# Q/K stacks of 16-row pieces, second tiles from token 768, and ten x tiles loaded during attention

## The chip, the core and the metric

The kernel runs on one core of a Trainium2 chip. Its engines work side by side: TensorE (PE; its weight loads are PEld), VectorE (DVE), ScalarE (ACT), GpSimd (POOL) and SyncE (SP), which here issues all DMA transfers, in an order written out by hand. The metric is device microseconds of one launch; lower is better.

## What is computed

A transformer block on x of 2048 tokens by 640, in float32: a layer norm, sliding-window attention, and a gated MLP that mixes over tokens.

```python
qkv = layernorm(x) @ wqkv                   # 32 heads of 20
scores = q @ k.T * 20 ** -0.5               # key at most 255 tokens back, not ahead
h = x + (softmax(scores) @ v) @ wo
z = gelu(layernorm(h) @ w_in)               # 640 -> 2 x 864
g = w_sp @ layernorm(z[:, 864:]) + b_sp     # over the 2048 tokens
out = h + (z[:, :864] * g) @ w_out
```

## The kernel before

Float32 products are made from pieces: a number is split into a high and a low part (`split`), and three products of parts are added up. For Q and K the parts are three bfloat16 numbers; six pairs of parts, 20 rows each, stand one above another in 120 rows, a *stack*, so that one bfloat16 matmul over 120 rows gives a score.

First the v projection, then Q and K. `qk_item(m, c)` makes block m (of 10, 128 rows each) for 512 tokens c; `split_qk` makes its three parts in `sg` (VectorE, ScalarE, GpSimd) and SP stores them to `qk_d` in DRAM (L619). `load_stack(g)` loads the stack of four heads (group g of 8) into one of three slots: two halves of 1024 tokens, 12 transfers of 20 rows each, every sixth row (L329). Slot 2 lies in `xb`, which held the normalized x.

Attention runs in 128 steps s, 16 to a group. `max_item` (L345) makes scores of 32-query strips and lets VectorE take their row maxima: one reduction (L369) that writes a throw-away tile `junk`, from a ring of two, and reads out the maximum into a column of `m_cols`. It runs 18 steps (`LEAD`) ahead of `score_item` (L391), which makes the transposed scores with the maxima as three more rows, and ScalarE's exponential. `max_rows` turns 32 columns of maxima and sends them through DRAM into the slot (L384, L386). `pv_item` (L425) multiplies by v; `o_d` gets the result through a ring of six tiles `ot` (L462). Where a window of keys or queries crosses token 1024, `tokens` cuts the matmul in two. Steps 0 to 109 have maxima and scores; the first 18 units of maxima run beside the last Q/K items, and in the last 18 steps no maxima are left.

Every engine but GpSimd takes its instructions in program order (`manual_schedule`). The waits between them follow from the tiles: a tile of a ring is reused when its last users are done, and reads and writes of the same bytes are ordered.

`last_steps` has what is done at the end of a step: from 117 on the first loads of the projection (`load_sums`, `load_o`), and the x tiles (`load_x2`) and half of w_in's first columns (`load_win_half`) from 121. `proj_early` loads the split wo. Then follow 16 tiles of `proj_o`, with `add_h` (h = x + projection, stored to `h_d`), a layer norm, and `turn_h` (stored to `hn_d`), while `win1_prep` splits w_in. The gated MLP follows, in a list of steps.

Of the kernel before, what the change touches and what calls it, by code (L numbers as in the profile page):

```python
# [34 lines left out]
def block_kernel(ctx, tc, x, xt, wqk, wv, wo, w_in, wsp, bsp, w_out, out):  # L35
# [16 lines left out]
    qk_d = dram.tile([2, 3, 2, 2 * DH, H // 2, S // 4], F32, name="qk_d")  # L52
# [73 lines left out]
    def open_early(pl):  # L126
# [4 lines left out]
        mem["xh"] = [pl.tile([P, D], F32, name=f"xh{i}") for i in range(6)]  # L131
        mem["ho"] = [pl.tile([P, D], F32, name=f"ho{i}") for i in range(3)]
        mem["wraw"] = pl.tile([P, 2, 2, HF], F32, name="wraw")
# [27 lines left out]
    def load_x2(i):  # L161
        hs[i] = mem["xh"][i % 6]
        nc.sync.dma_start(hs[i], x[i * P:(i + 1) * P, :])
# [75 lines left out]
    def ready(i):  # L239
# [7 lines left out]
        121: lambda: (load_x2(0), load_win_half(0, 0), load_x2(1), inverse_load(1), load_win_half(0, 1), ready(0)),  # L247
        122: lambda: first_sums(1),
        126: lambda: (ready(1), inverse_recip(1), inverse_store(1), load_o(2), inverse_load(2), load_x2(2)),
        127: lambda: (ready(2), norm_o(3), load_sums(2)),  # L250
        128: lambda: (split_o(3, True)(), inverse_recip(2), load_sums(3), inverse_store(2), load_o(3)),
        129: lambda: (load_x2(3), load_x2(4)),
    }


    with ExitStack() as ab:
# [7 lines left out]
        xb = [xb.tile([P, CH], F32R, name=f"xb{i}") for i in range(2)]  # L264
        s0 = pool(low0, "slot0p")
        s0 = [s0.tile([P, 2 * S], F32R, name=f"slot0_{i}") for i in range(2)]
# [12 lines left out]
        add_slot(2, [h[:, :2 * S] for h in xb])  # L279
# [36 lines left out]
        def load_stack(g):  # L316
# [3 lines left out]
            if g < 3:  # L320
                for h in st:
                    nc.gpsimd.memset(h[96:P, 1], ONES)
                    if g == 2:
                        yield
            for b in range(2):
                for j, parts in enumerate(((0, 0), (0, 1), (0, 2), (1, 0), (1, 1), (2, 0))):
                    for a in range(2):
                        src = qk_d[g // 4, parts[a], b, a * DH:(a + 1) * DH, g % 4 * 4:g % 4 * 4 + 4]
                        nc.sync.dma_start(st[b][j:6 * DH:6, a], src)  # L329
                        yield  # L330

        def tokens(st, rows, a, hh, t0, n):

            o = 0
            while o < n:
                c, t = divmod(t0 + o, S // 2)
                w = min(n - o, S // 2 - t)
                yield o, w, st[c][:rows, a, hh, t:t + w]
                o += w

        def one(st, rows, a, hh, t0, n):
            (_, _, x), = tokens(st, rows, a, hh, t0, n)
            return x

        def max_item(g, qb, hh, strips=True):  # L345
# [4 lines left out]
            n = (qb + 1) * P - lo  # L350
            keep = mask[:, 384 - n:]
            if strips:
# [3 lines left out]
                for j in range(4):  # L356
                    q0 = qb * P + 32 * j
                    for o, w, k in tokens(st, 120, 1, hh, lo + skip * j, n):
                        nc.tensor.matmul(ps[32 * j:32 * j + 32, o:o + w], one(st, 120, 0, hh, q0, 32), k,  # L359
                                         start=True, stop=True, tile_position=(0, 32 * j))  # L360
            else:
                for o, w, k in tokens(st, 120, 1, hh, lo, n):
                    nc.tensor.matmul(ps[:, o:o + w], one(st, 120, 0, hh, qb * P, P), k, start=True, stop=True)  # L363
# [3 lines left out]
            junk = tmp2.tile([P, 384], BF16, tag="junk", bufs=2, name=f"junk{g}_{qb}_{hh}")  # L367
# [4 lines left out]
        def max_rows(g, b):  # L372
# [13 lines left out]
            nc.sync.dma_start(slot_w[g % 3][b][120:123, 0], rows.rearrange("a (h r) c -> a h (r c)", h=4))  # L386
# [4 lines left out]
        def score_item(u, hh):  # L391
# [14 lines left out]
            for i in range(4):  # L406
# [4 lines left out]
                for o, w, q in tokens(st, 123, 0, hh, kb * P + b, e - b):  # L411
                    nc.tensor.matmul(ps[32 * i:32 * i + 32, b + o:b + o + w], one(st, 123, 1, hh, k0, 32), q,  # L412
                                     start=True, stop=True, tile_position=(0, 32 * i))
# [51 lines left out]
        if True:  # L465
# [3 lines left out]
            def load_x(i):  # L469
                xts[i] = tmp.tile([P, D], F32, tag="ta", bufs=3, name=f"xt{i}")  # L470
# [6 lines left out]
            def load_xt(i):  # L477
                tag, bufs = ("wql", 4) if i % 3 == 2 else ("tb", 2)
                xns[i] = tmp.tile([P, KD, P], F32, tag=tag, bufs=bufs, name=f"xt_t{i}")
# [18 lines left out]
            def xn_tile(i):  # L498
                return tmp.tile([P, D], F32, tag="tb", bufs=2, name=f"xn{i}")
# [6 lines left out]
            def store_std():  # L506
                ps = s2_tile()[:NT, :P]
                nc.tensor.transpose(ps, inv_std, ident)
                row = tmp.tile([NT, P], F32, tag="std", bufs=2, name="std_row")
# [44 lines left out]
            def load_wqk(m):  # L554
                raws[m] = tmp.tile([P, KD, P], F32, tag="wraw", bufs=3, name=f"wqraw{m}")
# [10 lines left out]
            def load_wo(k):  # L566
                raws[k] = tmp.tile([P, D], F32, tag="wraw", bufs=3, name=f"woraw{k}")
# [16 lines left out]
            def load_std(c):  # L584
                stds[c] = tmp.tile([P, 512], F32, tag="std", bufs=2, name=f"std{len(stds)}_{c}")
# [17 lines left out]
            def split_qk(m, c, ps):  # L603
                sg = tmp.tile([P, 3, 512], BF16, tag="ta", bufs=3, name=f"sg{m}_{c}")
                rest = tmp.tile([P, 512], F32, tag="tb", bufs=2, name=f"rest{m}_{c}")
# [11 lines left out]
                T = S // 4  # L617
# [945 lines left out]
```

## Time and profile before

| | us |
|---|---|
| median of 3 runs | 1105.15 (1104.84 to 1106.06) |
| the profiled execution | 1106.78 |
| its span | 1105.1 |
| attention with maxima and scores | 240.0 to 437.6 of the span |
| last attention steps | 437.6 to 462 |
| output projection, first norm | 462 to 547 |

In the profile L12 is line 12 of the kernel, `out<-in` are tiles without their numbers, `xN` counts instructions, and "idle before" is time in which the engine did nothing ahead of an instruction, with what ended it. "issue" is a wait that no semaphore explains. A row of a timeline has start, duration, engine, line and operation; a row of waits has the total, the number of times and the longest.

### The profile page before, as it was taken

The page shows a single profiled execution, that of the slowest core. Times are in us where ns is not written, and L with a number is a line of the kernel's source. Part 1 is how long each engine was busy: PE and PEld are TensorE (multiplying, and loading weights), DVE is VectorE, ACT ScalarE, POOL GpSimd, SP SyncE. Part 2 cuts the span into 40 slices and gives each one's busy share as a digit, 9 for nine tenths or more (in the row PEclk, how much of TensorE's full clock was granted, in tenths as well). Part 3 has the DMA queues.
Part 4 walks back from the last instruction along what each step waited for, and adds up shares of the span by engine and source line. Part 5 has one row for each costly group of instructions (what it writes and reads, how often), then busy time and mean ns, then how long its engine had stood idle before and what let it go on. Part 6 is the DMA issues. An engine that isn't in the chain of part 4 may idle for free.

```text
span 1105.1 us, 28747 instructions
## 1 busy us (share of the span) xinstructions
PE 1075.2 (97%) x11059; PEld 968.4 (88%) x11059; DVE 781.0 (71%) x2157; ACT 604.7 (55%) x1258; POOL 314.0 (28%) x447
## 2 busy tenths in 40 slices
PE   8999999999999999999999999999999999999998
PEld 8998886658888787699999998999999899999998
DVE  6643445779999897575677668655556899987684
ACT  4443443249999899756766556443458433333331
POOL 4324446677766666721200012000001000000000
PEclk9999999999999999999999999999999999999999
DMA  7834657555565565689655342242441467684642
GB/s 252 296 115 118 175 172 262 169 181 171 190 188 189 178 192 151 183 263 296 252 184 174 131 142 77 66 133 97 127 148 51 173 223 254 229 276 137 195 141 96
DMA packets 92281, 194.73 MB, mean 176 GB/s; under 512 B 11952, under 2 KB 46272, under 8 KB 88256
## 3 DMA queue, kind: packets, MB, share of 16 engines
q1 hardware_dynamic: 92144, 192.90, 53.4%
q8 instruction: 87, 1.43, 0.6%
q14 instruction: 50, 0.41, 0.1%
HBM read 127.90 MB, written 64.95 MB: 175 GB/s over the span
## 4 chain that ended last, share of the span: by engine, by line
PE 79%; DMA 6%; ACT 4%; DVE 4%; issue 4%; POOL 2%; SPq 1%; DVEq 0%; POOLq 0%; ACTq 0%
PE g L1181 23%; PE pv L440 6%; PE bank L359 5%; PE bank L412 5%; PE zb L1066 4%; PE qk L592 4%; PE qk L594 4%; PE qk L593 4%; PE out_x L1345 3%; PE zx L1006 2%; PE out_v L1345 2%; PE zv L1006 2%; DMA h_d<-xh 1%; PE zy L1006 1%; PE zw L1006 1%
## 5 line engine op out<-in xcount | busy, mean ns | idle before, releaser
L415 ACT ACTIVATE pt<-bank 128x384 f32<-128x384 f32 (+1 forms) x452 | 180.2, 483 | 17.2 <-PE bank L412 10.8
L1181 PE MATMUL g<-zl,aw 128*128 128x432 f32 x768 | 169.1, 357 | 1.5 <-ACT zl L828 1.0
L369 DVE CUSTOM_DVE_ANT_0 junk<-bank,strip 128x288 bf16<-128x288 f32 x392 | 156.1, 452 | 12.3 <-PE bank L359 10.1
L828 ACT ACTIVATE aw<-fx 128x512 fp32r<-128x512 f32 (+2 forms) x152 | 86.2, 587 | 127.6 <-DVE fx L822 57.9
L1181 PEld LDWEIGHTS g<-zl,aw 128*128 128x128 f32 x768 | 144.0, 188 | 8.1 <-ACT zl L828 1.4
L440 PE MATMUL pv<-pt,v_sb 128*32 128x192 f32 (+3 forms) x1984 | 135.2, 322 | 4.6 <-POOL pt L419 2.4
L822 DVE TENSOR_TENSOR aw<-fx,aw 128x512 fp32r<-128x512 f32 (+2 forms) x152 | 95.8, 638 | 60.1 <-ACT aw L828 59.8
L1181 PE MATMUL g<-ze,aw 128*128 128x432 f32 x576 | 132.6, 359 | 2.3 <-DVE row L822 2.3
L1181 PEld LDWEIGHTS g<-ze,aw 128*128 128x128 f32 x576 | 107.1, 188 | 9.0 <-DVE row L822 3.7
L419 POOL TENSOR_SCALAR_AFFINE_SELECT pt<-pt 128x512 f32<-128x512 f32 x128 | 83.5, 653 | 61.2 <-ACT pt L415 59.0
L412 PE MATMUL bank<-slot 123*32 123x288 bf16 (+8 forms) x1296 | 95.7, 273 | 2.0 <-issue 1.3
L359 PE MATMUL bank<-slot 120*32 120x288 bf16 (+6 forms) x1248 | 93.5, 275 | 0.9 <-DVE mcol L369 0.8
L440 PEld LDWEIGHTS pv<-pt,v_sb 128*32 128x32 f32 x1984 | 65.5, 110 | 11.9 <-POOL pt L419 6.2
L422 POOL TENSOR_SCALAR_AFFINE_SELECT pt<-pt 128x512 f32<-128x512 f32 x112 | 71.2, 635 | 0.0
L412 PEld LDWEIGHTS <-slot 123*32 123x32 bf16 x1728 | 58.8, 96 | 13.0 <-issue 3.6
L359 PEld LDWEIGHTS <-slot 120*32 120x32 bf16 x1408 | 52.1, 95 | 15.2 <-issue 7.2
L369 DVE CUSTOM_DVE_ANT_0 junk<-bank,mask 128x384 bf16<-128x384 f32 (+2 forms) x120 | 51.2, 444 | 17.0 <-PE bank L363 15.7
L822 DVE TENSOR_TENSOR row<-g,row 128x432 f32<-128x432 f32 x80 | 48.3, 603 | 21.0 <-PE g L1181 20.6
L616 POOL TENSOR_TENSOR sg<-rest,sg 128x512 bf16<-128x512 f32 x40 | 46.7, 1167 | 56.3 <-ACT sg L615 45.6
L606 DVE TENSOR_TENSOR rest<-qk,std 128x512 f32<-128x512 f32 x40 | 27.6, 690 | 44.9 <-PE qk L594 44.9
L608 ACT ACTIVATE sg<-rest 128x512 bf16<-128x512 f32 x40 | 25.2, 631 | 54.3 <-DVE rest L606 54.3
L118 PE MATMUL wo_ps<-xb,xb 128*128 128x320 f32 x260 | 52.4, 311 | 1.5 <-DVE mvc L1460 1.5
(263 smaller groups left out, 2538.4 us busy)
## 6 DMA issues: line engine op xcount, KB each, us to landing
slot<-qk_d SPq DMA_DIRECT2D x144, 160.0 KB
fx<-wsp_in SPq DMA_DIRECT2D x32, 512.0 KB
qk_d<-sg SPq DMA_DIRECT2D x40, 384.0 KB
o_d<-ot SPq DMA_DIRECT2D x64, 128.0 KB
xb<-qk_d SPq DMA_DIRECT2D x48, 160.0 KB
fx<-hn_d SPq DMA_DIRECT2D x24, 320.0 KB
z_d<-row SPq DMA_DIRECT2D x16, 432.0 KB
g_d<-row SPq DMA_DIRECT2D x16, 432.0 KB
```

Of the source, the lines that this page charges most:

```text
L359: nc.tensor.matmul(ps[32 * j:32 * j + 32, o:o + w], one(st, 120, 0, hh, q0, 32), k, start=True, stop=True, tile_position=(0, 32 * j))
L369: nc.vector.tensor_tensor_reduce(out=junk[:, :n], in0=ps[:, :n], in1=keep, scale=1.0, scalar=NEG, op0=OP.add, op1=OP.max, accum_out=m_cols ...
L412: nc.tensor.matmul(ps[32 * i:32 * i + 32, b + o:b + o + w], one(st, 123, 1, hh, k0, 32), q, start=True, stop=True, tile_position=(0, 32 * i))
L415: nc.scalar.activation(pt[:, hh, :n], ps[:, :n], AF.Exp, scale=SCALE)
L419: nc.gpsimd.affine_select(out=pt[:, :, :P], in_=pt[:, :, :P], pattern=[[0, 4], [1, P]], base=0, channel_multiplier=-1, compare_op=OP.is_ge ...
L422: nc.gpsimd.affine_select(out=pt[:, :, 256:], in_=pt[:, :, 256:], pattern=[[0, 4], [-1, P]], base=-1, channel_multiplier=1, compare_op=OP. ...
L440: nc.tensor.matmul(ps[32 * hh:32 * hh + 32, a - 512 * c:b - 512 * c], v_sb[:, kb, v0:v0 + 32], pt[:, hh, a - kb * P:b - kb * P], start=fir ...
L822: (eng or nc.vector).tensor_tensor(out=out, in0=a, in1=b, op=op)
L828: nc.scalar.activation(out, a, AF.Copy)
L1006: nc.tensor.matmul(ps, a[x], b[:, y], start=start and m + x + y == 0, stop=stop and m == n - 1 and x == 1, skip_group_check=True)
L1181: nc.tensor.matmul(ps, w[m][:, x, k], zc[k][m][:, y], start=start and k + x + y == 0, stop=stop and k == 3 and x == 1, skip_group_check=True)
L1345: nc.tensor.matmul(o[b][:, :HD], l[:, x, k * P:(k + 1) * P], r[k][:, y], start=start and k + x + y == 0, stop=stop and k == 2 and x == 1, ...
```

## The change

The rows of Q and K in the weights are reordered: of each head's 20 rows, the first 16 make eight blocks, the last 4 two more. A stack now has six pieces of 16 rows and one of 24 (the six times 4 last rows, which `split_qk` stores six times, as often as the pairs use them). The second tile of a stack starts at token 768 and holds 1280 tokens; the first keeps 1024. So no window crosses a seam, and `tokens` is gone. The three rows of maxima follow the two tiles.

A scratch `raw`, kept through attention, takes the place of several rings of the first stage (`tmp_of` counts them out). From step 66 it takes ten x tiles, each in two transfers of 64 rows, and from 106 w_in's first piece in transfers of 32 rows. The wo loads go in halves. The store of h is issued after the loads of its step. The ring of `junk` has one tile instead of two.

```diff
-    qk_d = dram.tile([2, 3, 2, 2 * DH, H // 2, S // 4], F32, name="qk_d")
+    WORDS = (S // 4, S // 4 + P)
+    qk_d = [dram.tile([2, 2, 3, 16, H // 2, n], F32, name=f"qk_d{b}") for b, n in enumerate(WORDS)]
+    qr_d = [dram.tile([2, 2, 6, DH - 16, H // 2, n], F32, name=f"qr_d{b}") for b, n in enumerate(WORDS)]
+    PAIRS = ((1, 0), (0, 1), (0, 0), (0, 2), (2, 0), (1, 1))
...
     def load_x2(i):
-        hs[i] = mem["xh"][i % 6]
-        nc.sync.dma_start(hs[i], x[i * P:(i + 1) * P, :])
+        hs[i] = mem["xh"][i % 10]
+        for r in ((slice(0, 64), slice(64, P)) if i < 10 else (slice(0, P),)):
+            nc.sync.dma_start(hs[i][r], x[i * P:(i + 1) * P][r])
...
-        nc.sync.dma_start(mem["wraw"][:, b], src[r:r + P])
+        for o in range(0, P, 32):
+            nc.sync.dma_start(mem["wraw"][o:o + 32, b], src[r + o:r + o + 32])
...
-                nc.sync.dma_start(wo_s[p][:, k].bitcast(F32), wo_d[k, p])
+                for r in (slice(0, 64), slice(64, P)):
+                    nc.sync.dma_start(wo_s[p][r, k].bitcast(F32), wo_d[k, p, r])
...
-        121: lambda: (load_x2(0), load_win_half(0, 0), load_x2(1), inverse_load(1), load_win_half(0, 1), ready(0)),
+        121: lambda: (inverse_load(1), ready(0)),
...
-        126: lambda: (ready(1), inverse_recip(1), inverse_store(1), load_o(2), inverse_load(2), load_x2(2)),
+        126: lambda: (ready(1), inverse_recip(1), inverse_store(1), load_o(2), inverse_load(2)),
...
-        129: lambda: (load_x2(3), load_x2(4)),
+        129: lambda: load_win(2),
     }
+    for i in range(10):
+        last_steps[66 + 4 * i] = lambda i=i: load_x2(i)
+    for b in range(2):
+        last_steps[106 + 4 * b] = lambda b=b: load_win_half(0, b)
...
+        raw = pool(base_stack, "raw").tile([P, 10 * D + 2 * FH], F32, name="raw")
+        mem["xh"] = [raw[:, i * D:(i + 1) * D] for i in range(10)]
+        mem["wraw"] = view(raw, 10 * D, 2, 2, HF)
...
-        s0 = [s0.tile([P, 2 * S], F32R, name=f"slot0_{i}") for i in range(2)]
+        s0 = [s0.tile([P, 8 * n], F32R, name=f"slot0_{i}") for i, n in enumerate(WORDS)]
...
+            q, heads = g // 4, slice(g % 4 * 4, g % 4 * 4 + 4)
             for b in range(2):
-                for j, parts in enumerate(((0, 0), (0, 1), (0, 2), (1, 0), (1, 1), (2, 0))):
+                for j, parts in enumerate(PAIRS):
                     for a in range(2):
-                        src = qk_d[g // 4, parts[a], b, a * DH:(a + 1) * DH, g % 4 * 4:g % 4 * 4 + 4]
-                        nc.sync.dma_start(st[b][j:6 * DH:6, a], src)
+                        nc.sync.dma_start(st[b][16 * j:16 * j + 16, a], qk_d[b][q, a, parts[a], :, heads])
                         yield
+                for a in range(2):
+                    nc.sync.dma_start(st[b][96:6 * DH, a], qr_d[b][q, a, :, :, heads].rearrange("j d h t -> (j d) h t"))
+                    yield
...
-                    for o, w, k in tokens(st, 120, 1, hh, lo + skip * j, n):
-                        nc.tensor.matmul(ps[32 * j:32 * j + 32, o:o + w], one(st, 120, 0, hh, q0, 32), k,
-                                         start=True, stop=True, tile_position=(0, 32 * j))
+                    nc.tensor.matmul(ps[32 * j:32 * j + 32, :n], one(st, half_b, 120, 0, hh, q0, 32),
+                                     one(st, half_b, 120, 1, hh, lo + skip * j, n),
+                                     start=True, stop=True, tile_position=(0, 32 * j))
...
-            junk = tmp2.tile([P, 384], BF16, tag="junk", bufs=2, name=f"junk{g}_{qb}_{hh}")
+            junk = tmp2.tile([P, 384], BF16, tag="junk", bufs=1, name=f"junk{g}_{qb}_{hh}")
...
+            if b == 0:
+                nc.sync.dma_start(st[0][120:123, 0], rows)
+                nc.sync.dma_start(st[1][120:123, 0, :, :P], rows[:, :, 6 * P // 2:])
+            else:
+                nc.sync.dma_start(st[1][120:123, 0, :, P:], rows)
...
-                for o, w, q in tokens(st, 123, 0, hh, kb * P + b, e - b):
-                    nc.tensor.matmul(ps[32 * i:32 * i + 32, b + o:b + o + w], one(st, 123, 1, hh, k0, 32), q,
-                                     start=True, stop=True, tile_position=(0, 32 * i))
+                c = int(kb > 5)
+                nc.tensor.matmul(ps[32 * i:32 * i + 32, b:e], one(st, c, 123, 1, hh, k0, 32),
+                                 one(st, c, 123, 0, hh, kb * P + b, e - b),
+                                 start=True, stop=True, tile_position=(0, 32 * i))
...
-                xts[i] = tmp.tile([P, D], F32, tag="ta", bufs=3, name=f"xt{i}")
+                xts[i] = tmp_of("ta")[:, :D]
...
+                for b in range(2):
+                    t0, t1 = max(c * 256, 3 * P * b), min(c * 256 + 256, (3 * P + WORDS[1]) if b else WORDS[0])
...
+                    if m % 5 < 4:
...
+                        nc.sync.dma_start(bass.AP(tensor=base.tensor, offset=base.offset,
+                                                  ap=[[W, P], [16 * n * W, 3], [1, t1 - t0]]), part)
+                        continue
+                    for a in range(2):
+                        for p in range(3):
+                            js = [j for j, x in enumerate(PAIRS) if x[a] == p]
...
-            for _ in range(1 + s % 2 if s >= NT else 2 * min(s, 1)):
+            for _ in range(1 + (s % 4 > 0) if s >= NT else 2 * min(s, 1)):
                 next(ld, None)
...
-        nc.sync.dma_start(h_d[i], hs[i])
+        return hs[i]
...
-        if i == 1:
-            load_win(2)
-        if 1 < i < NT - 3:
-            load_x2(i + 3)
+        if 2 < i < NT - 7:
+            load_x2(i + 7)
+        nc.sync.dma_start(h_d[i - 1], hx)
```

The calls of `load_stack`'s pieces in the first stage go from three to four at a time.

More of the change, by code (lines that the diff above doesn't have):

```diff
@@ L278, in block_kernel @@
         add_slot(0, s0)
-        add_slot(2, [h[:, :2 * S] for h in xb])
+        add_slot(2, [h[:, :8 * n] for h, n in zip(xb, WORDS)])
         mask = tmp2.tile([P, 384], BF16, name="mask")
@@ L357, in max_item @@
                     q0 = qb * P + 32 * j
[L358 to L363 removed]
+                    nc.tensor.matmul(ps[32 * j:32 * j + 32, :n], one(st, half_b, 120, 0, hh, q0, 32),
+                                     one(st, half_b, 120, 1, hh, lo + skip * j, n),
+                                     start=True, stop=True, tile_position=(0, 32 * j))
+            else:
+                nc.tensor.matmul(ps[:, :n], one(st, half_b, 120, 0, hh, qb * P, P), one(st, half_b, 120, 1, hh, lo, n),
+                                 start=True, stop=True)
             b, c = divmod(qb, 8)
@@ L498, in xn_tile @@
             def xn_tile(i):
-                return tmp.tile([P, D], F32, tag="tb", bufs=2, name=f"xn{i}")
+                return tmp_of("tb")
             def mean_row(i):
@@ L508, in store_std @@
                 nc.tensor.transpose(ps, inv_std, ident)
-                row = tmp.tile([NT, P], F32, tag="std", bufs=2, name="std_row")
+                row = tmp_of("std")[:NT, :P]
                 nc.scalar.activation(row, ps, AF.Copy)
@@ L566, in load_wo @@
             def load_wo(k):
[L567 removed]
+                raws[k] = tmp_of("wraw")
                 nc.sync.dma_start(raws[k], wo[k * P:(k + 1) * P, :])
@@ L718, in block_kernel @@
                 if n >= 20:
-                    for _ in range(3):
+                    for _ in range(4):
                         next(ld0, None)
@@ L730, in dense_tail @@
                         s1 = pool(x01, "slot1p", side="right")
-                        add_slot(1, [s1.tile([P, 2 * S], F32R, name=f"slot1_{i}") for i in range(2)])
+                        add_slot(1, [s1.tile([P, 8 * n], F32R, name=f"slot1_{i}") for i, n in enumerate(WORDS)])
                     if n >= 7:
-                        for _ in range(3):
+                        for _ in range(4):
                             next(ld1, None)
@@ L739, in block_kernel @@
                 if n % 5 == 4:
-                    for _ in range(3):
+                    for _ in range(4):
                         next(ld0, None)
@@ L752, in block_kernel @@
                     next(rows)
-            assert next(dense, 0) == 0 and next(ld0, 0) == 0
+            assert next(dense, 0) == 0 and next(ld0, 0) == 0 and next(ld1, 0) == 0
             for _ in after[0]:
@@ L1544 @@
     w = np.asarray(A_wqkv).reshape(D, 3, H, DH)
-    wqk = w[:, :2].reshape(D, 2, 2, H // 2, DH).transpose(2, 1, 4, 0, 3).reshape(2 * D // P, 8, KD, P, H // 2)
+    wqk = w[:, :2].reshape(D, 2, 2, H // 2, DH).transpose(2, 1, 4, 0, 3)
+    wqk = np.concatenate([wqk[:, a, d] for d in (slice(0, 16), slice(16, DH)) for a in range(2)], axis=1)
+    wqk = wqk.reshape(2 * D // P, 8, KD, P, H // 2)
     wqk = wqk.transpose(0, 3, 2, 1, 4).reshape(2 * D // P, P, KD, P)
```

58 lines of the change are left out of this document (33 added, 25 removed).

## The prediction

> **What bounds the kernel now.** I read the busy shares of the page first, then the stretches of the span, then, for the attention stretch, the groups, the order of time and the waits of one engine after the other.
>
> ```profile
> PE 1075.2 (97%) x11059; PEld 968.4 (88%) x11059; DVE 781.0 (71%) x2157; ACT 604.7 (55%) x1258; POOL 314.0 (28%) x447
> q8 instruction: 87, 1.43, 0.6%
> ```
> ```profile
> 178.00:240.00 62.00, 61.31 (x290) 38.43 (x289) 44.45 (x157) 17.25 (x28) 39.55 (x37) 1.00 0.58 195
> 240.00:437.60 197.60, 188.42 (x5682) 158.79 (x5681) 184.31 (x939) 180.54 (x467) 138.58 (x236) 1.00 0.57 179
> 437.60:462.00 24.40, 22.27 (x582) 14.44 (x578) 10.13 (x17) 23.92 (x44) 20.80 (x33) 1.00 0.63 165
> 462.00:547.00 85.00, 80.50 (x588) 78.88 (x589) 59.14 (x127) 50.46 (x94) 20.59 (x34) 1.00 0.84 268
> ```
>
> TensorE is busy 97% of the span, so on the whole it is the bound. The second fence says where that is not the whole story (columns: length, then PE, PEld, DVE, ACT, POOL busy, clock, DMA share, GB/s). In 240.0 to 437.6, attention with row maxima and scores side by side, PE is busy 188.4 us of 197.6, and DVE 184.3 us: VectorE is 13.3 us short of full. Anything that adds a tenth to VectorE's work there makes it the bound. In the other three stretches VectorE has 17.6, 14.3 and 25.9 us to spare. So I look at what VectorE does in attention.
>
> ```profile
> L369 DVE CUSTOM_DVE_ANT_0 junk<-bank,strip 128x288 bf16<-128x288 f32 x392 | 156.1, 452 | 12.3 <-PE bank L359 10.1
> L369 DVE DVE_READ_ACCUMULATOR2_ANT mcol<- 128x1 f32 x443 | 36.1, 81 | 0.0
> L369 DVE CUSTOM_DVE_ANT_0 junk<-bank,mask 128x256 bf16<-128x256 f32 (+1 forms) x51 | 15.6, 349 | 0.0
> L461 DVE COPY ot<-pv 128x256 f32<-128x256 f32 x26 | 10.8, 414 | 0.0
> L378 DVE TENSOR_SCALAR m<-bank 32x128 bf16<-32x128 f32 x13 | 3.6, 276 | 0.5
> ```
> ```profile
> 330.53 0.45 DVE L369 CUSTOM_DVE_ANT_0 junk<-bank,strip 128x288 bf16<-128x288 f32 x1
> 330.90 0.08 DVE L369 DVE_READ_ACCUMULATOR2_ANT mcol<- 128x1 f32 x1
> 330.90 0.46 DVE L369 CUSTOM_DVE_ANT_0 junk<-bank,strip 128x288 bf16<-128x288 f32 x1
> 331.28 0.08 DVE L369 DVE_READ_ACCUMULATOR2_ANT mcol<- 128x1 f32 x1
> ...
> 336.07 0.27 DVE L378 TENSOR_SCALAR m<-bank 32x128 bf16<-32x128 f32 x1
> 336.38 0.28 DVE L379 SCALAR_TENSOR_TENSOR mr<-bank,m 32x128 f32<-32x128 f32 x1
> 336.59 0.44 DVE L369 CUSTOM_DVE_ANT_0 junk<-bank,strip 128x288 bf16<-128x288 f32 x1
> ...
> 337.34 0.41 DVE L461 COPY ot<-pv 128x256 f32<-128x256 f32 x1
> 337.68 0.43 DVE L369 CUSTOM_DVE_ANT_0 junk<-bank,strip 128x288 bf16<-128x288 f32 x1
> ```
>
> One row maximum is two instructions: the reduction, which writes a throw-away tile `junk`, and the read of its accumulator. A reduction takes 0.45 us, but the next one starts 0.37 to 0.38 us after it (330.53, 330.90, 331.28), at the same moment as the accumulator read of the one before. The reader is to see that overlap: each reduction starts before the one ahead of it is done, so it can't be waiting for it. With `junk` in a ring of two it has to wait for the last but one.
>
> **The change, part by part.** *The ring of `junk` goes from two tiles to one* (L367). Every reduction then writes bytes that the reduction just ahead writes. The tiles of a ring are handed on by waits, so each reduction must now wait for the accumulator read of the one before it; behind it on VectorE everything stands in order. What such a wait costs between two VectorE instructions is shown where one reads what the last wrote:
>
> ```profile
> 457.15 0.82 DVE L200 CAST xb<-m 128x640 fp32r<-128x640 f32 x1
> 458.00 0.87 DVE L203 TENSOR_TENSOR xb<-m,xb 128x640 fp32r<-128x640 f32 x1
> ...
> 478.03 0.82 DVE L203 TENSOR_TENSOR xb<-m,xb 128x640 fp32r<-128x640 f32 x1 [0.79 <-ACT xb L202]
> 478.77 0.82 DVE L194 TENSOR_TENSOR m<-m,rs 128x640 f32<-128x640 f32 x1
> ...
> 481.47 0.08 DVE L1460 DVE_READ_ACCUMULATOR2_ANT mvc<- 128x1 f32 x1
> 481.59 0.15 DVE L98 TENSOR_SCALAR mvc<-mvc 128x1 f32<-128x1 f32 x1
> ```
>
> The dependent pair (457.15, 458.00) starts 0.85 us apart, the independent one (478.03, 478.77) 0.74. After an accumulator read the instruction that needs it starts 0.12 us after the read's start. So the step from one reduction to the next lies between 0.377 + 0.12 = 0.50 us, and 0.452 + 0.081 + 0.04 = 0.57 us, where nothing overlaps. I take 0.57: a reduction waits for its bank from TensorE as well, and the second wait is one more step of VectorE's sequencer that L98 does not have. For the 51 shorter ones, whose overlap of 0.08 I take to be the same, it is 0.27 + 0.12 = 0.39, or 0.349 + 0.081 + 0.04 = 0.47.
>
> The stretch by VectorE alone: 392 x 0.57 + 51 x 0.47 = 247.4 us. A copy of L461 between two reductions takes 0.34 us (337.34 to 337.68), of which 0.19 lies in the wait: 26 x 0.15 = 3.9. The pair L378, L379 takes 0.52 (336.07 to 336.59) and hides 0.19 too: 13 x 0.33 = 4.3. Sum 255.6 us, against 197.6: **+58 us**. At the low end, 392 x 0.50 + 51 x 0.39 + 26 x 0.22 + 13 x 0.40 = 226.8: +29. For the high end I allow 0.02 us more a reduction: +66. Four reductions to a step make 2.28 us, where TensorE's four maxima, four scores and value products fill 197.6 / 110 = 1.8 us at most, so TensorE can't stay the bound. Before 240 us only 69 of the 512 reductions run (8 groups x 16 x 4, less 443), and 69 x 0.19 = 13 us fits in 17.6: nothing, 0 to +3.
>
> *Second tiles from token 768.* Windows that crossed token 1024 were two matmuls a strip and become one. This takes instructions from TensorE in steps 6 and 7 of each group of sixteen, which matters for its stalls:
>
> ```profile
> PE bank L359 <- issue: 3.7, 5, 1.2
> PE pv L440 <- issue: 1.6, 3, 1.1
> PE bank L412 <- issue: 1.3, 1, 1.3
> ```
> ```profile
> 425.51 0.21 PE L359 MATMUL bank<-slot,slot 120*32 120x96 bf16 x3 [0.88 <-issue]
> ```
>
> In 245 to 437.6 PE waits 6.6 us for "issue", nothing that the profile shows; one such wait ends on a split matmul (`slot,slot`, 425.51). The page's 87 transfers of instructions, 1.43 MB, make a late instruction fetch the likely cause. If VectorE is the bound these stalls are hidden behind it: worth nothing in my sum, and 6.6 us, with 1 us by my estimate for the matmuls themselves, if it is not.
>
> *Loads and stores of the stacks.*
>
> ```profile
> L329 SPq DMA_DIRECT2D slot<-qk_d x144: 694/703/1202, 160.5 to 412.3; - x144
> L619 SPq DMA_DIRECT2D qk_d<-sg x40: 359/366/422, 93.4 to 244.7; - x40
> ```
>
> Stack loads go from 24 to 28 a group (192 to 224), stores from 40 to 100: five pieces for each of ten blocks, those of the two last-rows blocks times six. A load of 20 rows takes SP 0.70 us, a store of 128 rows 0.36. For 16 rows no row shows the price: at 0.36 SP issues 81 us of loads instead of 135, at 0.70 157. The 60 more stores add 22 us on SP between 93 and 245 us. Behind them stand the loads of the scale rows, of weights and of the first stack, for which TensorE waits directly; twelve stores follow one another for the block that crosses the seam (4.3 to 8.4 us). The code leaves about one block (3.4 us of PE) of slack, so I put +1 us, 0 to +5. A row of maxima takes three transfers instead of two in 8 of 16 cases; they have ten steps. 0.
>
> *Ten x tiles and the first piece of w_in early, wo in halves, w_in in quarters.* Twenty and eight issues on SP from step 66 to 110, at 0.36 to 0.70 us; SP has the time, as steps get longer. 0. In the stretch after attention they are missing, and so is about 4.1 MB (10 x 320 KB + 864 KB) of 268 GB/s x 85 us = 22.8 MB.
>
> ```profile
> PE wo_ps L118 <- DVE mvc L1460: 3.7, 3, 1.7
> PE ht_ps L946 <- ACT hn L109: 0.7, 1, 0.7
> ...
> DVE m L194 <- DMA rs<-r_d: 7.9, 3, 4.0
> ```
>
> PE waits 4.4 us there, and VectorE ahead of it 7.9 us for the row sums, behind other transfers. I take -2.5 us, between -4.4 (all of it) and +1.5 (w_in's second piece is eight issues where it was two, ahead of the same row sums). The store of h moves behind the loads of its step on SP; its reader comes hundreds of us later: 0. The scratch that all these share is one tile whose parts are ordered by their bytes: 0.
>
> Sum: +58 + 1 - 2.5 = +56.5 us. The profiled execution took 1106.78 us (span 1105.1); it would become 1163. The median of the runs is 1.6 us below the profiled one: 1105.15 + 56.5 = 1161.7.
>
> **The rivals.** *The ring of one costs nothing*: no wait is set between two writes of one engine that nobody reads, or it is free. TensorE stays the bound, the stalls go with the split matmuls, and the time is 1105.15 - 6.6 - 1 - 2.5 + 1 = 1096. It decides from a step under 0.42 us: 443 of these with the 8 us around them are then no longer than the stretch is now. For it speaks that nothing reads `junk`; against it the 0.11 and 0.12 us above, and that a ring exists at all.
>
> [...]
>
> *The early loads spoil what the split gave*: no wait for `junk`, but stalls of 6.6 us remain since 4.1 MB more go through the queues in attention, and the stores cost what the later stretch gains: 1104 to 1107, no change.
>
> *The stores alone are late*: no wait for `junk`, stalls remain, and TensorE stands at 178 us for the first stack, +5 us: 1110.
>
> **How the numbers follow.** The wait of `junk` 0.82; a free ring 0.13; spoiled 0.03; late stores 0.02. No change means within 0.2%, 2.2 us, about what a measurement can tell here. So faster 0.13, same 0.03, slower 0.84. The first case's own range is +29 - 4.4 = +24.6, with a little under it for the short reductions, to +66 + 1.5 + 5 + 3 = +75.5: 1128 to 1180. It holds 0.80 by itself, so it is the range.
>
> **What would show it.** Right: the reductions of L369 start 0.5 to 0.6 us apart, and no longer with the accumulator read of the one before; VectorE is over 95% busy or waits only on itself in attention, PE is busy 75 to 85% there, waiting for `mcol` of L369; attention takes 255 us, and the stretches after it shift. Row sums are waited for less than 7.9 us after attention. Wrong: reductions 0.38 us apart as now (then the free ring, and "issue" waits of PE under 2 us settle whether it is 1096 or no change); or PE idle before 240 us by more than 3 us (the stores).

## The result, and the profile after

The change makes the kernel slower: 1213.74 us (1212.54 to 1216.22), 1.099 times the kernel before, interval 1.097 to 1.102. The profiled execution took 1212.54 us, its span 1210.8. The forecast had the direction, not the size: +56.5 us, within +23 to +75; it was +108.75 by the medians (1213.74 for 1104.99), and +105.7 in span.

Four stretches of the span, marked in each trace by the start of the first and of the last exponential of the scores (L415, after: L435) and by the first matmul of the projection. The columns are start and end, length, busy time of PE, PEld, DVE, ACT and POOL, granted clock, DMA share and GB/s. Rows of the stretches after:

```profile
178.00:270.80 92.80, 68.52 (x314) 42.41 (x315) 49.62 (x173) 20.63 (x34) 46.15 (x40) 0.86 0.97 194
270.80:548.00 277.20, 231.43 (x5305) 153.44 (x5308) 210.47 (x927) 212.59 (x479) 140.73 (x241) 0.98 0.84 158
548.00:568.80 20.80, 18.77 (x456) 11.14 (x445) 9.24 (x13) 20.37 (x32) 18.00 (x28) 1.00 0.60 162
568.80:653.00 84.20, 80.45 (x591) 79.33 (x592) 60.02 (x130) 50.57 (x93) 20.44 (x33) 1.00 0.73 228
```

And with the same marks before:

```profile
178.00:240.90 62.90, 61.77 (x302) 38.76 (x304) 45.35 (x161) 17.88 (x29) 40.45 (x37) 1.00 0.58 194
240.90:441.40 200.50, 191.66 (x5772) 161.19 (x5769) 184.30 (x937) 183.46 (x478) 140.70 (x242) 1.00 0.57 179
```

Up to the first score +29.9 us (270.8 for 240.9), attention +76.7 (277.2 for 200.5), the step into the projection +0.1, all after it -1.0. The sum is the 105.7 us of the span. What the two lost differs. In attention TensorE is busy 83% and waits, mostly for one line. Ahead of it, from 178 us on, it stands for 24.3 us where it stood for 1.1 before: twice for over 7 us, once for 6.7 us up to the first exponentials, and its granted clock falls (0.86 on average). Waits in attention, then ahead of it, then three stretches of 10 us around the ends of the two longest waits (184.8 and 195.5 us):

```profile
PE bank L372 <- DVE mcol L383: 34.1, 150, 1.7
```
```profile
PE bank L376 <- DMA slot<-qr_d: 7.8, 1, 7.8
PE qk L614 <- DVE raw L628: 7.4, 1, 7.4
PE bank L431 <- ACT pt L435: 6.7, 1, 6.7
```
```profile
180.00:190.00 10.00, 2.90 (x6) 1.82 (x6) 1.29 (x2) 1.52 (x3) 3.47 (x3) 0.66 1.03 204
190.00:200.00 10.00, 4.50 (x13) 2.68 (x14) 0.90 (x6) 1.26 (x2) 2.30 (x2) 0.55 1.11 182
200.00:210.00 10.00, 10.00 (x46) 6.32 (x46) 6.48 (x25) 2.52 (x4) 3.96 (x4) 0.93 0.98 167
```

Transfers got worse: the share of time in which the DMA engines are busy in attention went from 0.57 to 0.84, while the rate fell from 179 to 158 GB/s. That is not the longer stretch alone: the kernel before with a ring of one (e1 below) has an attention as long, with its old transfers:

```profile
241.20:517.10 275.90, 233.35 (x5776) 156.02 (x5779) 212.82 (x939) 215.22 (x479) 141.65 (x242) 1.00 0.42 130
```

There the share is 0.42 at 130 GB/s. No step of the prediction has dearer transfers.

### The profile page after: what moved, and what is told of

Read it like the earlier page. It is cut to its first block, busy times and chain, and to the rows that moved or that the text cites. A ratio compares the mean times of both kernels' runs of the same rounds, so it can differ in the third digit from the quotient of the medians.

```text
span 1210.8 us, 27993 instructions
## 1 busy us (share of the span) xinstructions
PE 1120.6 (93%) x10571; PEld 962.8 (80%) x10571; DVE 809.8 (67%) x2157; ACT 633.2 (52%) x1258; POOL 316.1 (26%) x447
## 4 chain that ended last, share of the span: by engine, by line
PE 40%; DMA 6%; DVE 4%; ACT 3%; issue 1%; SPq 1%; POOL 0%; DVEq 0%; ACTq 0%; POOLq 0%
PE g L1219 21%; PE zb L1104 4%; PE out_x L1383 3%; PE zx L1044 2%; PE out_v L1383 2%; PE zv L1044 2%; DMA rs<-r_d 1%; DMA m<-o_d 1%; PE zy L1044 1%; PE zw L1044 1%; DMA fx<-wsp_in 1%; PE out_y L1383 1%; PE yt L1338 1%; DVE row L860 1%; PE wo_ps L121 1%
## 5 line engine op out<-in xcount | busy, mean ns | idle before, releaser
L435 ACT ACTIVATE pt<-bank 128x384 f32<-128x384 f32 (+1 forms) x452 | 206.7, 472 | 64.6 <-PE bank L431 49.9
L383 DVE CUSTOM_DVE_ANT_0 junk<-bank,strip 128x288 bf16<-128x288 f32 x392 | 178.8, 456 | 64.0 <-PE bank L372 11.2
L460 PE MATMUL pv<-pt,v_sb 128*32 128x192 f32 (+3 forms) x1984 | 128.1, 324 | 1.9 <-POOL pt L442 0.8
L372 PE MATMUL bank<-slot 120*32 120x288 bf16 (+2 forms) x1248 | 97.2, 295 | 29.0 <-DVE mcol L383 25.2
L372 PEld LDWEIGHTS <-slot 120*32 120x32 bf16 x1248 | 60.2, 96 | 80.0 <-issue 64.8
L431 PE MATMUL bank<-slot 123*32 123x288 bf16 (+4 forms) x1296 | 99.0, 285 | 6.8 <-ACT pt L435 6.7
L630 ACT ACTIVATE raw<-raw 128x512 bf16<-128x512 f32 x40 | 25.2, 631 | 80.9 <-DVE raw L628 31.1
L638 POOL TENSOR_TENSOR raw<-raw 128x512 bf16<-128x512 f32 x40 | 46.6, 1165 | 60.3 <-ACT raw L637 57.6
L628 DVE TENSOR_TENSOR raw<-qk,raw 128x512 f32<-128x512 f32 x40 | 27.5, 689 | 45.6 <-PE qk L616 36.4
L431 PEld LDWEIGHTS <-slot 123*32 123x32 bf16 x1536 | 44.1, 97 | 11.5 <-issue 7.3
```

What stands on the lines that cost most here:

```text
L372: nc.tensor.matmul(ps[32 * j:32 * j + 32, :n], one(st, half_b, 120, 0, hh, q0, 32), one(st, half_b, 120, 1, hh, lo + skip * j, n), start=T ...
L383: nc.vector.tensor_tensor_reduce(out=junk[:, :n], in0=ps[:, :n], in1=keep, scale=1.0, scalar=NEG, op0=OP.add, op1=OP.max, accum_out=m_cols ...
L431: nc.tensor.matmul(ps[32 * i:32 * i + 32, b:e], one(st, c, 123, 1, hh, k0, 32), one(st, c, 123, 0, hh, kb * P + b, e - b), start=True, sto ...
L435: nc.scalar.activation(pt[:, hh, :n], ps[:, :n], AF.Exp, scale=SCALE)
L460: nc.tensor.matmul(ps[32 * hh:32 * hh + 32, a - 512 * c:b - 512 * c], v_sb[:, kb, v0:v0 + 32], pt[:, hh, a - kb * P:b - kb * P], start=fir ...
```

## The experiments

Line numbers differ by a few between kernels. All runs, by the same marks (us of the profiled span; ratio to the kernel before, with its interval). "Spread" is every sixth partition, "late" the old places of the loads of x, w_in and wo.

| kernel | to first score | attention | after it | ratio |
|---|---|---|---|---|
| before | 240.9 | 200.5 | 663.7 | 1 |
| after | 270.8 | 277.2 | 662.8 | 1.099 (1.097 to 1.102) |
| e1 before, ring of one | 241.2 | 275.9 | 661.3 | 1.070 (1.068 to 1.072) |
| e2 after, ring of two | 271.0 | 259.9 | 671.3 | 1.091 (1.088 to 1.095) |
| e3 e2, spread | 256.5 | 222.3 | 666.6 | 1.040 (1.037 to 1.043) |
| e19 e2, every second | 256.5 | 220.0 | 665.8 | 1.039 (1.035 to 1.043) |
| e7 after, spread | 257.6 | 274.0 | 662.2 | 1.080 (1.077 to 1.084) |
| e4 e2, late | 271.0 | 257.4 | 661.8 | 1.081 (1.078 to 1.084) |
| e12 after, late | 270.3 | 276.5 | 661.4 | 1.095 (1.093 to 1.097) |
| e5 e3, late | 256.7 | 209.7 | 662.6 | 1.023 (1.019 to 1.026) |
| e10 e5, fewer stores | 248.4 | 209.5 | 664.7 | 1.016 (1.014 to 1.019) |
| e18 e5, two more edits | 253.1 | 209.2 | 663.5 | 1.022 (1.019 to 1.025) |
| e8 before, side by side | 247.8 | 221.7 | 664.7 | 1.025 (1.019 to 1.030) |
| e9 split at 768 alone | 241.8 | 211.7 | 662.1 | 1.012 (1.007 to 1.016) |
| e13 e9, two a step | 241.2 | 220.4 | 665.9 | 1.018 (1.015 to 1.020) |
| e14 e13, early loads | 241.3 | 224.9 | 667.3 | 1.030 (1.027 to 1.034) |
| e15 e9, rows later | 241.7 | 202.8 | 663.5 | 1.003 (1.001 to 1.006) |
| e16 before, rows later | 241.8 | 204.1 | 660.1 | 1.002 (1.000 to 1.004) |

**The ring by itself (e1).**

```diff
-            junk = tmp2.tile([P, 384], BF16, tag="junk", bufs=2, ...)
+            junk = tmp2.tile([P, 384], BF16, tag="junk", bufs=1, ...)
```

> The kernel before with one edit: the throw-away tile of the reductions in a ring of one. If the wait between reductions is the whole of the lengthening of attention (277 us after, 198 before), reductions go at a pitch of 0.61 us as in the changed kernel and the time is about 1105 + 78 = 1183, with the stages before attention as they were. If the prediction's step of 0.57 us holds and the rest of the pitch comes from the new loads, it is 1105 + 58 = 1163. If the wait costs nothing and the pitch has another cause, 1105.

1180.1 us, against 1102.6 of the kernel before measured along with it: +77.5. Between the profiled executions attention is 75.4 us longer and the rest 2.1 us shorter. VectorE's timeline:

```profile
345.20 0.08 DVE L369 DVE_READ_ACCUMULATOR2_ANT mcol<- 128x1 f32 x1
345.43 0.46 DVE L369 CUSTOM_DVE_ANT_0 junk<-bank,strip 128x288 bf16<-128x288 f32 x1
345.81 0.08 DVE L369 DVE_READ_ACCUMULATOR2_ANT mcol<- 128x1 f32 x1
346.04 0.46 DVE L369 CUSTOM_DVE_ANT_0 junk<-bank,strip 128x288 bf16<-128x288 f32 x1
...
347.64 0.08 DVE L369 DVE_READ_ACCUMULATOR2_ANT mcol<- 128x1 f32 x1
347.64 0.42 DVE L461 COPY ot<-pv 128x256 f32<-128x256 f32 x1
347.98 0.45 DVE L369 CUSTOM_DVE_ANT_0 junk<-bank,strip 128x288 bf16<-128x288 f32 x1
```

The next reduction starts 0.23 us after the accumulator read's start (345.20 to 345.43), so the step is 0.61 us in place of 0.38; a copy that needs nothing from it starts with the read (347.64). Four reductions make 2.44 us a step, more than the 1.82 us that a step took before (200.5 / 110). The one edit is the ring, so its wait is shown, and it is the whole of the 77 us.

**The ring taken out of the change (e2).**

```diff
-            junk = tmp2.tile([P, 384], BF16, tag="junk", bufs=1, ...)
+            junk = tmp2.tile([P, 384], BF16, tag="junk", bufs=2, ...)
-            mr = tmp2.tile([32, P], F32, tag="mr", bufs=2, ...)
+            mr = tmp2.tile([32, P], F32, tag="mr", bufs=1, ...)
```

> The changed kernel with the throw-away tile in a ring of two again (a small tile of the row maxima is in a ring of one to make room). If the wait of the ring is what attention lost, the step of the reductions is 0.38 us again and attention takes 190 to 200 us. Then some 31 us of stalls ahead of attention remain: 1213.7 - 78 = 1136. If the stalls ahead of attention have their cause in the ring as well (the last of them stand beside the first reductions), 1105 or less.

1203.8 us: only 10 us came back. Attention takes 259.9 us with VectorE no longer in the way. A second bound stood right behind the first:

```profile
271.00:530.90 259.90, 206.63 (x5305) 167.61 (x5308) 187.10 (x927) 187.72 (x479) 140.83 (x241) 0.95 0.89 162
```
```profile
PE pv L460 <- issue: 19.7, 9, 3.9
PE bank L431 <- ACT pt L435: 8.6, 3, 8.2
PE bank L431 <- issue: 7.7, 4, 3.2
PE bank L372 <- DMA slot<-qk_d: 6.6, 3, 3.3
PE bank L372 <- issue: 6.0, 4, 2.8
```

The DMA engines are busy 0.89 of the stretch at 162 GB/s. TensorE waits 33.4 us for "issue", which was 6.6 before, and 10.3 us for the stack (the 8.2 us of the second line lie mostly ahead of the stretch). So my first rival (a free ring gives 1096) had the wrong price too.

**Where the rows lie (e3, e19, e7, e8).**

```diff
-                        nc.sync.dma_start(st[b][16 * j:16 * j + 16, a], ...)
+                        nc.sync.dma_start(st[b][j:96:6, a], ...)                                      # e3, e7
+                        nc.sync.dma_start(st[b][32 * (j // 2) + j % 2:32 * (j // 2) + 32:2, a], ...)  # e19
```

> As the changed kernel with a ring of two, and each piece of 16 rows written to every sixth partition, as the kernel before wrote its 20, in place of 16 partitions side by side. Theory of the packets: 16 partitions side by side make each 8 KB packet take about twice as long, so that stores and loads land late; spread out, the DMA share in attention falls from about 0.9 to 0.6 and the stalls ahead of attention go: 1100 to 1112. Theory of SP's queue: the 60 remainder stores at 0.58 us each hold up the scale rows and the stack loads whatever the packets take: within 5 us of the kernel with a ring of two alone, 1130 to 1136.

> As the kernel with a ring of two (16 rows side by side, 1203.8) and the one with rows on every sixth partition (1147.5), with the 16 rows of a piece on every second partition of 32 here. [...] If what counts is only how far rows lie apart in SBUF, it is nearer to side by side: 1180 to 1200.

The same bytes in as many transfers: 1147.5 and 1148.1 us, 56 us less than e2. Attention of e3, then of e19, then e3's waits for "issue":

```profile
256.50:478.80 222.30, 196.16 (x5304) 159.39 (x5307) 183.82 (x927) 185.01 (x479) 141.13 (x242) 0.96 0.72 194
```
```profile
257.00:475.00 218.00, 194.09 (x5268) 158.45 (x5271) 183.44 (x927) 182.99 (x474) 139.72 (x241) 0.96 0.73 195
```
```profile
PE bank L372 <- issue: 1.6, 2, 1.0
PE bank L431 <- issue: 1.1, 1, 1.1
PE pv L460 <- issue: 0.5, 2, 0.3
```

The share falls from 0.89 to 0.72 and the rate rises to 194 GB/s; "issue" falls from 33.4 to 3.2 us. By the trace's DMA records an 8 KB packet takes 0.71 us on average side by side (e2), 0.50 on every sixth and 0.49 on every second partition; before, 20 rows on every sixth, 0.41. (The averages include the last rows, which stay side by side in all three.) Rows that lie two apart do as well as rows six apart, so how far apart rows lie does not decide; why rows side by side are dearer, no run shows. Nor is lying side by side the whole measure: in e8, next, 20 rows lie side by side as well, and a packet takes 0.51 us. In its records a median of 10 packets of a stack are in flight when one starts, 13 in e2; that this is the reason is my reading, and no run tests it.

> The kernel before with one edit: each stack load writes its 20 rows to 20 partitions side by side in place of every sixth one; same count, same bytes, same order. If partitions side by side are what makes packets slow, 8 KB packets go from about 0.4 to 0.75 us, DMA share in attention from 0.58 to 0.85 or more, and the time from 1103 to 1130 to 1165. If it takes 16 rows (or pieces of two tensors) to make them slow, no change: 1103.

```diff
-                        nc.sync.dma_start(st[b][j:6 * DH:6, a], src)
+                        nc.sync.dma_start(st[b][20 * j:20 * j + 20, a], src)
```

The kernel before with this edit: 1134.5 us for 1106.0, +28. The packets took 0.51 us and the DMA share of attention is 0.61, both less than I expected, and the time still came within the expected range. TensorE's waits in attention:

```profile
PE bank L359 <- issue: 15.1, 7, 3.9
PE pv L440 <- issue: 4.0, 2, 2.7
PE bank L412 <- issue: 2.1, 1, 2.1
```

21.2 us for "issue" in place of 6.6, with nothing changed but the place of rows: this wait of TensorE depends on the transfers (e2 and e3 say the same). It does not go by the DMA share: e3 has a share of 0.72 and waits 3.2 us, e8 0.61 and 21.2. It is long in the three kernels that have rows side by side and a ring of two (33.4 us in e2, 42.1 in e4, 21.2 in e8), and at most 7.8 us in all others. The DMA records join it to instructions: over the attention of all profiles, 91 waits for "issue" are longer than 0.3 us, and 89 of them end 1.2 to 1.9 us after a 16 KB packet of the instruction queue (q8) has landed; with 41 to 45 such packets in an attention, chance would give about one in six. The packets themselves are no slower (1.22 us on average before, 1.11 in e8, 1.33 in e2), so if they are late, they are late ahead of their start, where the records show nothing.

> The changed kernel with one edit, the rows of 16 spread over every sixth partition; the ring of one stays. If the ring and the slow transfers are two bounds on the same stretch, of which the longer one counts, attention stays at 276 us and only the stages ahead of it gain 14: 1198 to 1200. If the two add up, it is the kernel with spread rows and a ring of two plus 77: 1225, more than the changed kernel itself, so at most 1214. If the ring hid all that transfers cost, also ahead of attention: 1180.

1194.7 us: attention 274.0, the stages ahead of it 13 us shorter. The ring and the transfers are bounds beside each other, of which the longer counts: mending one alone gives 10 us (e2) or 19 (e7), both together 66 (e3).

**The stages ahead of attention (e10, e18).** The place of the rows was worth 14.5 of the 29.9 us (e2 to e3); most of the 6.7 us wait went with it (2.1 in e3). There ScalarE's exponentials stand behind a split of the last Q/K block (L630), which waits 4.9 us for a store to `qk_d` to land. e3 left 15.6 us. SP after:

```profile
154.49 9.71 SPq L656 DMA_DIRECT2D qr_d<-raw  x12
164.29 0.53 SPq L608 DMA_DIRECT2D raw<-rstd_d  x1
...
169.64 5.87 SPq L656 DMA_DIRECT2D qr_d<-raw  x6
...
177.96 0.36 SPq L608 DMA_DIRECT2D raw<-rstd_d  x1
```
```profile
DVE raw L628 <- DMA raw<-rstd_d: 7.2, 2, 4.4
L656 SPq DMA_DIRECT2D qr_d<-raw x60: 468/584/1370, 147.1 to 279.2; - x60
```

Twelve remainder stores hold SP for 9.7 us, and a scale row that VectorE needs stands behind them; VectorE waits 2.8 us for it. Six more stores and four stack loads follow ahead of the next scale row, issued at 177.96 us. VectorE waits 4.4 us for that one, and TensorE's 7.4 us end with it. e10 (from e5) leaves something out: all six copies hold the first part, so the last rows of the second and third parts are missing from its sums.

```diff
-                        for p in range(3):
-                            js = [j for j, x in enumerate(PAIRS) if x[a] == p]
...
+                        nc.sync.dma_start(bass.AP(..., ap=[[W, 64], [4 * n * W, 6], [1, t1 - t0]]),
+                                          part[64 * a:64 * a + 64, 0:1].to_broadcast([64, 6, t1 - t0]))
```

> The kernel with a ring of two, spread rows and late loads (1130.7), whose first stage ends 16 us later than before. Here each remainder block is stored by two stores of six copies in place of six (20 issues in place of 60, the same bytes and packets); all six copies hold the first part, so the second and third parts' last rows are left out of the sums. If what is late there is SP's queue, 60 issues at 0.58 us with the scale rows behind them, the waits of TensorE at 177 us (4.4) and 185 us (5.4) shrink and the first scores come 8 to 13 us earlier: 1118 to 1122. If it is the bytes and packets of the copies, or the late landing of the remainder rows, no change: 1128 to 1132.

1122.9 us, with the first score 8.3 us earlier. Of TensorE's two waits (5.4 and 4.4 us in e5) one of 5.6 us is left. So half of what remained is the number of stores, at 0.58 us each on SP. e10 has a third as many, at 0.63 us. e18 (from e5) keeps the stores, loads each scale row once, and moves the row maxima as in e15 below:

```diff
-                stds[c] = tmp_of("std")
+                if c in stds:
+                    return
+                stds[c] = raw[:, 5504 + 512 * c:6016 + 512 * c]
```

> The changed kernel with its costs taken away one by one: ring of two, rows spread, late loads (1130.7 so far), and here also the load of the row maxima two steps later, and each scale row loaded once into four tiles of the scratch in place of again for every pair of blocks. If TensorE's two waits ahead of attention come from scale rows behind the remainder stores on SP, the first scores come 8 to 14 us earlier than at 256.7; if the waits of SP for the row maxima are behind the stalls of attention, that is 198 to 203 us in place of 210: in all 1104 to 1115. If neither, 1128 to 1132.

1127.7 us, the third of my cases: only 3.6 us came back ahead of attention, and little in it. One of TensorE's two waits went; the other, for the first remainder rows, grew from 5.4 us (e5) to 9.1. It, and SP where these rows are loaded:

```profile
PE bank L369 <- DMA slot<-qr_d: 9.1, 1, 9.1
```
```profile
178.53 3.94 SPq L651 DMA_DIRECT2D qr_d<-raw  x6
182.52 0.97 SPq L344 DMA_DIRECT2D slot<-qr_d  x2
```

The load stands behind remainder stores on SP whatever the scale rows do. So the scale rows are one place where SP's lateness shows, not its cause. The other 7.5 us (248.4 in e10 against 240.9) may lie in the landing of the remainder rows or in their bytes; nothing here tells which.

**The early loads (e4, e5, e12).** Undone, whole, at the old places:

```diff
-        121: lambda: (inverse_load(1), ready(0)),
+        121: lambda: (load_x2(0), load_win_half(0, 0), load_x2(1), inverse_load(1), load_win_half(0, 1), ready(0)),
...
-        if 2 < i < NT - 7:
-            load_x2(i + 7)
+        if 1 < i < NT - 3:
+            load_x2(i + 3)
```

> As the changed kernel with a ring of two, but x tiles, w_in's pieces and wo are loaded whole and where the kernel before loads them. If the early loads help the projection stage as predicted, this is 2.5 us slower than the kernel with a ring of two alone (0 to 4.4). If they get in the way of the stack loads in attention or of the waits behind w_in's second piece, it is up to 5 us faster.

> As the kernel with a ring of two and spread rows (1147.5), with x, w_in and wo loaded whole and late as before the change. With rows side by side late loads were worth 12 us (1203.8 to 1191.9). If the early loads cost by the bytes they add to queues that are behind in attention, the queues being less behind now they cost 3 to 8: 1140 to 1144. If they cost the same whatever the rest does: 1135. If they cost only where queues are full and else help as predicted: 1148 to 1150.

> The changed kernel (ring of one, rows side by side) with x, w_in and wo loaded whole and late. With a ring of two, late loads were worth 12 us (rows side by side) and 17 us (rows spread). If the ring of one covers in attention what the early loads cost there, only the stages after attention count: 1211 to 1216. If the early loads cost as much as with a ring of two: 1197 to 1202. By the prediction's term, 2.5 us slower: 1216.

Late is faster each time: by 12 us (e4 against e2), 17 (e5 against e3) and 3.7 (e12 against the changed kernel, about what the intervals can tell; there the ring covers most of it). None of e5's expectations went as far as its 1130.7. In e2, 9.5 of the 12 us lie after the last exponential of L435, where the last scores wait for their row of maxima. SP issues its load at 540.6 us, right behind four pieces of w_in; neither wait is in e4:

```profile
PE pair L431 <- DMA slot<-m_d: 5.8, 1, 5.8
PEld L431 <- DMA raw<-w_in_in: 6.3, 1, 6.3
```

In e3 most of it lies in attention (222.3 us, and 209.7 in e5), where x tiles stand between the stack loads. In the projection they bring nothing: the first 580 matmuls of it take 82.8 us with them and 82.6 without (e12), for 84.0 before the change, and the row sums are still waited for 6.6 us (5.9 in e12).

**The split at 768 alone (e9, e13, e14, e15, e16).** e9 has 20 rows on every sixth partition from one tensor, ring of two, late loads: of the change the second tile from 768 is left, with the shared scratch `raw` and the later store of h. (Like all kernels from e2 on that come from the changed one with a ring of two, it has the row maxima's `mr` in a ring of one; e15, which has it too, shows that it costs little.)

```diff
-    qk_d = [dram.tile([2, 2, 3, 16, H // 2, n], F32, name=f"qk_d{b}") for b, n in enumerate(WORDS)]
-    qr_d = [dram.tile([2, 2, 6, DH - 16, H // 2, n], F32, name=f"qr_d{b}") for b, n in enumerate(WORDS)]
+    qk_d = [dram.tile([2, 3, 2 * DH, H // 2, n], F32, name=f"qk_d{b}") for b, n in enumerate(WORDS)]
...
-                        nc.sync.dma_start(st[b][16 * j:16 * j + 16, a], qk_d[b][q, a, parts[a], :, heads])
+                        src = qk_d[b][q, parts[a], a * DH:(a + 1) * DH, :, :][:, heads]
+                        nc.sync.dma_start(st[b][j:6 * DH:6, a], src)
```

> Second tiles from token 768 alone: 20 rows to every sixth partition as before, one tensor, 50 stores in place of 40 and 24 loads a group (12 of them 25% larger), ring of two, late loads. If the split is worth what the prediction put on it once nothing else is late (6.6 us of stalls for instructions and 1 us of matmuls): 1095 to 1098. If the larger loads or stores cost as much: 1103 to 1108. If the first stage's loss came from the split itself (a second tile needs its rows a quarter earlier) and not from the remainder stores: 1115 or more.

1118.3 us, 12 slower: no gain. The first stage is as before, which also says that its 29.9 us came from pieces and remainder, not from the split or the scratch. Waits of SP in attention, and SP around one of them:

```profile
SPq L395 <- DMA m_d<-m: 14.0, 6, 3.6
SPq L392 <- DMA m_d<-m: 10.8, 7, 3.4
```
```profile
276.10 0.36 SPq L388 DMA_DIRECT2D m_d<-m  x1
276.56 0.39 SPq L472 DMA_DIRECT2D o_d<-ot  x1
280.61 0.74 SPq L395 DMA_DIRECT2D slot<-m_d  x1
```

SP stands 3.7 us with nothing issued until the store of the row maxima has landed. A group of some 28 us needs 24 x 0.71 + 8 x 0.4 + 2.5 (the row maxima's own) = 23 us of SP, and these waits, 24.8 us in seven groups, add 3.5 us to each.

> The kernel with the split at 768 alone (1118.3), whose attention has a wait of 2 to 3 us in the sixth step of each group, where the first maxima of the next group's second tile come. Here SP issues two pieces a step in place of three in two steps, so the second tile is issued four steps (7 us) earlier. If those waits are late landing of the second tile, attention goes from 212 to 198 us or less: 1100 to 1105. If they are waits for the row of maxima or for instructions, 1115 to 1120.

```diff
-            for _ in range(1 + s % 2 if s >= NT else 2 * min(s, 1)):
+            for _ in range(2 * min(s, 1)):
                 next(ld, None)
```

1124.4 us, 6 slower than e9. Issuing the second tile earlier did not help: TensorE still waits 5.1 us for stack loads (3.5 in e9), and scores wait longer for the row of maxima:

```profile
PE bank L421 <- DMA xb<-m_d: 5.9, 2, 3.0
PE bank L421 <- DMA slot<-m_d: 4.7, 3, 2.2
```

That is 10.6 us, where e9 has 5.8 (4.9 and 0.9).

> As the last, with the early loads of the change (x tiles, w_in's first piece, wo in halves, in small transfers during attention). If they cost by meeting the stack loads in the queues, 5 to 15 us more than the last: 1108 to 1118. If they cost only where the stack loads are late, and the second tile is now early, they bring the 2.5 us that the prediction gave them: 1098 to 1102.

1136.2 us, 12 more by the medians (5.9 between the profiled executions, of which e13's was its slowest): early loads cost here too, with neither the ring of one nor rows side by side. Now the line of the row maxima (e15 from e9, e16 from the kernel before):

```diff
-                if hh == 3 and u1 % 8 == 1 and s <= NU - LEAD + 1:
+                if hh == 3 and u1 % 8 == 3 and 1 < s <= NU - LEAD + 3:
                     next(rows)
```

> The split at 768 alone (1118.3) with one line moved: the load of a group's row maxima into its stack is issued two steps later than its store. SP waits there for the store to land (1.3 to 4 us each time), with stack loads behind it. Theory: with the split, SP has no slack left in a group (24 issues at 0.74 us, eight stores of values, two such waits), lags TensorE by some 7 us, and the row or the second tile comes late in the sixth step. Then with the waits of SP gone the lag goes and attention falls from 212 towards 198: 1100 to 1106. If the transfers themselves are late (bytes), 1115 to 1120.

> The kernel before with the same one line moved. If the stalls for nothing that the profile shows in its attention (6.6 us) are fetches of instructions, no change: 1102 to 1106. If SP's waits for the row of maxima lie behind some of them, 2 to 5 us faster: 1098 to 1102.

e15 takes 1108.2 us, 10 less than e9; attention 202.8, and SP's waits for these stores fell from 24.8 to 1.3 us. So some 10 of the 12 us of the split alone were SP's waits. e16 shows no gain on the kernel before, where SP waits 15.9 us for these stores; why that costs nothing there is not shown. TensorE's longest waits in e15's attention:

```profile
PE bank L421 <- issue: 4.2, 3, 1.6
PE bank L421 <- DMA slot<-m_d: 3.0, 3, 1.4
PE pv L450 <- issue: 2.0, 2, 1.6
```

6.2 us of "issue" are left, about as many as before the change (6.6), with no split matmul in the kernel. No version here beats the kernel before.

## Why the prediction was right and wrong

By its own steps; the terms that missed add up to 105.7 - 56.5 = 49.2 us.

- *The ring of `junk`, +58 (+29 to +66).* The mechanism was right: TensorE waits for `mcol`, VectorE is the bound, `junk` is what it waits for. The step was mis-sized: 0.61 us, not 0.57. The row I took for it (L98, 0.12 us after an accumulator read's start) is a small instruction without the sequencer's row (EVENT_SEMAPHORE, 21 ns) that 480 of the 512 reductions have ahead of them in the trace before the change; the reduction starts 0.23 after (e1). In the changed kernel the stretch is +76.7: 18.7 us missing.
- *Loads and stores, +1 (0 to +5).* This step failed: +29.9, 28.9 missing. I saw the twelve stores ahead of the scale row and put them at 4.3 to 8.4 us (9.7 measured), but set them alone against a slack of one block: 24 remainder stores stand on SP between 147 and 176 us, and TensorE waits for the scale row behind the last six. And I priced transfers only by what SP takes to issue them. On SP the pieces of 16 rows are cheap as hoped (0.42 us); in the queues they are dear, by where their rows lie (0.71 us a packet in e2, 0.50 in e3). The code showed the 16 rows side by side in place of every sixth, and I did not cost it: spread, they give back 14.5 us ahead of attention (e3), fewer stores another 8.3 (e10), and some 7 stay open. My own sign of being wrong came: TensorE idle ahead of attention, by 24.3 us.
- *The early loads, -2.5.* Sign wrong in every pair of kernels. In the changed kernel most of the cost is hidden under the ring, so this missed 1.5 us in the sum (-1.0 for all that follows attention). The -1.0 is not theirs: without them (e12) it is -2.3. "SP has the time: 0" held; the queues did not have it.
- *The split, hidden, else worth 6.6 + 1.* Hidden, as said. The "else" was wrong: with the ring of two, late loads and SP's waits gone (e15), the stalls for "issue" are still there, so they do not hang on the split matmuls. The prediction guessed late instruction fetches; the DMA records fit that (89 of 91 such waits end 1.2 to 1.9 us after an instruction packet has landed, under e8).
- *The rivals.* "Ring of one costs nothing" is refuted by e1, and its 1096 by e2. "Early loads spoil" and "late stores" named mechanisms that are there (12 to 17 us for the early loads with a ring of two, 8.3 of the 29.9 us ahead of attention for the number of stores), with prices far too small and only as cases without the ring's wait.
- *The range* added ends of terms that were each taken from SP's and VectorE's rows. A term without a row (how long a 16-row packet takes) had no width at all.

## What to carry to other kernels

When a transfer's shape changes, price three things: its issue on the queue, who stands behind it there, and how its rows fall on the partitions; here the last made a packet take 0.71 us in place of 0.50 (e2, e3). The 1 KB packets of other transfers in attention took 0.08 us on average in the changed kernel, 0.05 before. A long wait can cover a second bound: here one that lengthened attention by 75.4 us (e1) covered one of 59.4 (e2, 259.9 for 200.5), so the value of removing it is read only with it removed. The second tile of a ring that VectorE writes at every reduction was worth 77.5 us in the kernel before (e1), though nobody reads it.

## What the runs showed of the hardware that was not expected

- Sixteen rows of 8 to 10 KB side by side in SBUF: DMA share 0.89 at 162 GB/s in attention (e2); the same on every second partition 0.73 at 195 (e19).
- TensorE's waits for "issue" depend on where the rows of other transfers land: 6.6 us before, 21.2 with only the rows moved (e8), 33.4 (e2), 3.2 (e3). They end with instruction packets: 89 of 91 such waits end 1.2 to 1.9 us after a packet of q8 landed.
- After an accumulator read, a reduction that waits for it starts 0.23 us after the read's start (e1); one that doesn't starts with it (before the change, 330.90 us).
- Around waits of 7.4 and 7.8 us ahead of attention (they end at 184.8 and 195.5 us) the granted clock averaged 0.66, 0.55 and 0.93 in the three stretches of 10 us from 180 us on. A matmul from 178 us to the first score took 0.218 us on average (68.52 / 314), 0.205 before (61.77 / 302): by this estimate some 4 of the 29.9 us.
